# Powers as three 8-bit parts for the decay masks, and a second tile pool at the same place modulo 2048

## The chip, the core and the metric

The kernel runs on one core of a Trainium2 chip. It uses five engines: TensorE (PE, with its weight loads shown apart as PEld), VectorE (DVE), ScalarE (ACT), GpSimd (POOL) and SyncE (SP, which here only issues transfers). The metric is the device time of one execution in microseconds; a kernel's time is the median of its runs.

## What is computed

Three stages in a row: a retention attention with a decay per head, and two feed-forward blocks. Cut to what matters here:

```python
# q, k, v: 2 x 8 heads x 768 x 64; lam: one decay per head, 0.97 to 0.99
Dmask = np.where(rel >= 0, lam[:, None, None] ** rel[None, :, :], 0.0)
for b in range(nb):
    intra = np.einsum('bhij,bhjd->bhid', (qb @ kb.T) * Dmask, vb)
    inter = np.einsum('bhid,bhde->bhie', qb * lam_pow, kv_state)
    out[:, :, sl] = intra + inter
    kv_state = lam_block * kv_state + (kb * rev_pow).T @ vb
x = out                                    # 1536 tokens x 512
h = x @ w_in                               # 512 -> 2048
g = np.where(h >= 1, h, np.where(h <= -1, 0, (h + 1) ** 2 / 4))
x = g @ w_out
return ((x @ w_a) * (x @ w_b)) @ w_out2    # 512 -> 1536 -> 512
```

All of it is in 32 bits. The kernel takes attention in chunks of 128 tokens, so its masks hold powers of lam from 0 to 127.

## The kernel before

The kernel writes down every operation as a step with the engines that can do it, a cost for each, and the buffers that it reads and writes (`Plan.step`). `Plan.place` then gives each step an engine, a start and a buffer, by these costs and by a due time that follows from TensorE's steps; the program is emitted in that order, and the hardware follows it with semaphores. A change of costs or steps near the start therefore plans the whole program anew.

The buffers: 26 + 8 working tiles ("t" and "early", 128x512 32-bit words), 40 tiles for operands of products ("r"), 4 for raw weights ("raw"), three activation blocks ("block"), 7 banks of PSUM ("ps"). When attention is over, the 8 early tiles are given back, and eight more operand tiles ("late") take their place: early and late are the second pool. Between the first tiles and the second pool lie small constants, each a column of 64 bytes (`column`).

At the start the kernel makes its tables. GpSimd raises lam to exponents that lie along the partitions (`power`, L408): partitions 0 to 31 hold lam^c, 32 to 63 lam^(16c), 64 to 95 lam^(c-16) with zeros where c < 16 (L413 to L415, on VectorE). Tiles of ones and zeros (`ones_where`, `near` and `far`, L419 to L437, made by VectorE from an iota of GpSimd) pick for each key position its power: TensorE multiplies a 32x128 piece of such a tile with the 32x8 powers, 8 times into bank f1 (the far table), 16 times each into f2 and f3 (the near tables), L464 to L471. One more product spreads powers for the queries over all partitions (bank bt, L472). ScalarE copies f1 and bt out; `masks` (L483 to L493) makes from f1, f2 and f3 the two masks on VectorE and GpSimd; `query_powers` (L495) fills the query table on GpSimd.

`warm` (L510) offers 40 filler steps, each of two products of a zero tile with 512 columns; the plan puts as many where TensorE would stand idle before the first feed-forward product ends, and drops the rest. They write into a bank that they share with others. Attention then runs over twelve chunks: scores (L530), masked scores (`att_mask`), state update, output (`att_out`), and from the fifth chunk on it is interleaved with the first feed-forward products, which are "wide": 128x128 weights, 512 columns, twelve to a group. From about 99 us on only wide products are left.

Helpers record most operations, so many have one line: all products L347, two-operand instructions L328, copies and casts L332, loads L343. Operand names in a row are output<-moving operand,weights for products.

Of the kernel before, what the change touches and what calls it, by code (L numbers as in the profile page):

```python
# [9 lines left out]
F32 = mybir.dt.float32  # L10
F32R = mybir.dt.float32r
BF16 = mybir.dt.bfloat16
# [68 lines left out]
class Plan:  # L81
# [56 lines left out]
    def place(self, free, late, closes, ends, lookahead, reserve):  # L138
# [7 lines left out]
        lag, port, dma, side = 0.0, {"DVE": 0.0, "POOL": 0.0}, 0.0, 0.0  # L146
# [58 lines left out]
        while waiting:  # L205
# [24 lines left out]
            if len(way) > 3:  # L230
                if e == "SP":
                    dma = max(dma, begin + 1.4) + way[3] / 375e3
                    s.end = dma + 0.5
                else:
                    side = max(side, begin + 1.4) + way[3] / 190e3
                    dma = max(dma, begin + 1.4) + way[3] / 375e3
                    s.end = side + 0.5
            else:
                s.end = s.done + (0.2 if e == "PE" else 0.0)
# [27 lines left out]
def retention_ffn_kernel(ctx: ExitStack, tc: tile.TileContext, lam, att, w1i, w1o, w2ab, w2o, out):  # L267
# [104 lines left out]

    def column(name, dtype=F32):
        return View(fixed([128, 16], dtype, name))

    def small(e, o, ins, emit, cost=0.17, **kw):
# [3 lines left out]
    lamb, kdf, powers = column("lamb").of(lambda t: t[:, 0:H]), column("kdf").of(lambda t: t[:, 0:H]), column("powers")  # L380
    half, qi, ci, qf, cf, ef, keep, pi, dg = (
        column(n, I32 if n in ("qi", "ci", "pi") else F32)
        for n in ("half", "qi", "ci", "qf", "cf", "ef", "keep", "pi", "dg")
    )
    one = lambda v: v.of(lambda t: t[:, 0:1])
    rows32 = lambda v, i, n=1: v.of(lambda t: t[32 * i:32 * (i + n)])
    powers8 = powers.of(lambda t: t[:, 0:H])
    idle = new().of(lambda t: t.bitcast(BF16)[:, 0:512])
    load(lamb, bass.AP(tensor=lam.tensor, offset=lam.offset, ap=[[0, 128], [1, H]]), 4096, [("ACT", 2.2, False, 4096)])
    small("POOL", one(qi), [], lambda: nc.gpsimd.iota(one(qi)(), pattern=[[0, 1]], base=0, channel_multiplier=1), 0.14)  # L390
    small("DVE", idle, [], lambda: nc.vector.memset(idle(), 0.0), 0.3)
    small("DVE", one(ci), [one(qi)],
          lambda: ts_(out=one(ci)(), in0=one(qi)(), scalar1=31, scalar2=None, op0=ALU.bitwise_and))
    small("DVE", one(cf), [one(ci)], lambda: nc.vector.tensor_copy(one(cf)(), one(ci)()))
    small("DVE", one(qf), [one(qi)], lambda: nc.vector.tensor_copy(one(qf)(), one(qi)()))

    def exponents():
        nc.vector.tensor_copy(one(ef)(), one(cf)())
        x, y = (one(v)()[32:64] for v in (ef, cf))
        ts_(out=x, in0=y, scalar1=16.0, scalar2=None, op0=ALU.mult)  # L400
        x, y = (one(v)()[64:96] for v in (ef, cf))
        ts_(out=x, in0=y, scalar1=-16.0, scalar2=0.0, op0=ALU.add, op1=ALU.max)

    small("DVE", one(ef), [one(cf)], exponents, 0.51)

    def power(o, e):
# [3 lines left out]
    power(powers8, ef)  # L410
    power(kdf, qf)
    small("DVE", one(keep), [one(cf)],
          lambda: ts_(out=one(keep)(), in0=one(cf)(), scalar1=16.0, scalar2=None, op0=ALU.is_ge))  # L413
    small("DVE", powers8, [powers8, one(keep)],
          lambda: ts_(out=powers8()[64:96], in0=powers8()[64:96], scalar1=one(keep)()[64:96], scalar2=None, op0=ALU.mult))  # L415
# [3 lines left out]
    def ones_where(pattern, base, dtype=F32):  # L419
        n = new()  # L420
        whole = i_(n)
        small("POOL", whole, [], lambda: nc.gpsimd.iota(whole(), pattern=pattern, base=base, channel_multiplier=0), 0.7)

        def equal(shift):
            o, c = new(), column(f"c{base}_{shift}")
            small("DVE", one(c), [one(cf)],
                  lambda: ts_(out=one(c)(), in0=one(cf)(), scalar1=float(-shift), scalar2=None, op0=ALU.add))
            plan.step([("DVE", dve())], [o], [whole, one(c)],
                      lambda e: ts_(out=o(), in0=whole(), scalar1=one(c)(), scalar2=None, op0=ALU.is_equal))
            return o  # L430

        return equal

    equal = ones_where([[1, 4], [0, 8], [1, 16]], 1)
    near = [equal(4 * g) for g in range(4)]
    equal = ones_where([[1, 4], [1, 8], [0, 16]], -8)
    far = [equal(4 * g) for g in range(2)]  # L437
# [11 lines left out]
    def numbers():  # L449
        nc.gpsimd.iota(wi()[:, 0:8], pattern=[[1, 8]], base=32, channel_multiplier=0)  # L450
        nc.gpsimd.iota(wi()[:, 8:24], pattern=[[1, 16]], base=1, channel_multiplier=0)
# [8 lines left out]
    small("DVE", spread, [powers8, held], lambda: nc.vector.tensor_tensor(  # L460
        out=by_head(spread()[:, 0:192]), in0=powers8().rearrange("p (h o) -> p h o", o=1).to_broadcast([128, H, 24]),
# [3 lines left out]
    for o, q, sel in ((f1, 1, far), (f2, 0, near), (f3, 2, near)):  # L465
        kws = []
        for i in range(4 * len(sel)):
            kws.append(dict(out=o.of(lambda t, i=i: t[:, i * H:(i + 1) * H]),
                            lhsT=sel[i // 4].of(lambda t, i=i, q=q: t[32 * q:32 * q + 32, (i % 4) * 128:(i % 4 + 1) * 128]),
                            rhs=rows32(powers8, q), start=True, stop=True))  # L470
        mm(kws, 0.07 * len(kws), [o], [powers8, *sel])  # L471
    mm([dict(out=cols(bt, 0, 192), lhsT=full.of(lambda t: t[0:64, 0:128]), rhs=spread.of(lambda t: t[0:64, 0:192]),  # L472
             start=True, stop=True)], 0.35, [bt], [full, spread])
# [29 lines left out]

    masks(0)
# [470 lines left out]
```

## Time and profile before

| | |
|---|---|
| median of 3 runs | 614.87 us (614.62 to 616.12) |
| the profiled execution | 615.42 us |
| its span, first to last instruction | 613.6 us |
| TensorE busy | 602.4 us, 98% |
| VectorE, ScalarE, GpSimd busy | 63%, 46%, 74% |
| DMA queue of the loads | 50.86 MB, 24.1% of 16 engines' span |

TensorE is busy for nearly the whole span, and the other engines are not. Records of products overlap: a product's duration holds its way through the array, so the distance of one group's start to the next is the time that the group costs. Idle time of the other engines costs nothing unless TensorE waits for them. The "granted clock" of the views is the share of TensorE's full clock of 2.4 GHz.

### The profile page before, as it was taken

To read this page: it belongs to the slowest core of one execution; us is meant where nothing else is said; L and a number is where in the kernel's file an instruction comes from. 1 tells how busy PE (TensorE), PEld (TensorE's weight loads), DVE (VectorE), ACT (ScalarE), POOL (GpSimd) and SP (SyncE) were. 2 spreads that over 40 slices of the span, in tenths; PEclk is the share of its full clock that TensorE was granted. 3 is DMA by queue.
4 is the path that set the end of the run, shared out by engine and by line. 5 is a ranking of instruction groups with operands and counts; after the bars stand their busy time and mean duration, and the time that the engine had idled before them with its cause. 6 is when DMAs were issued, how large, how long until landed. Compare 5 with 4: busy or idle time off the path is not lost.

```text
span 613.6 us, 8555 instructions
## 1 busy us (share of the span) xinstructions
PE 602.4 (98%) x3140; PEld 494.8 (81%) x3140; DVE 389.4 (63%) x621; ACT 283.7 (46%) x498; POOL 453.2 (74%) x397
## 2 busy tenths in 40 slices
PE   6999999999999999999999999999999999999996
PEld 5887878888888888888888888888888888888885
DVE  3378884515897588677887645463873774764454
ACT  0064655644854375337766465431542542542410
POOL 4277579996979496949799999774777778768730
PEclk9999999999999999999999999999999999999999
DMA  8446530120403041304023221211121212210006
GB/s 296 182 143 240 193 136 17 69 68 2 137 19 120 1 138 34 104 0 138 0 70 109 98 68 69 69 35 34 70 73 66 69 68 69 69 70 0 1 35 204
DMA packets 19193, 51.93 MB, mean 85 GB/s; under 512 B 2256, under 2 KB 3280, under 8 KB 19152
## 3 DMA queue, kind: packets, MB, share of 16 engines
q1 hardware_dynamic: 18432, 50.86, 24.1%
q10 hardware_dynamic: 720, 0.53, 0.3%
q8 instruction: 24, 0.39, 0.3%
q14 instruction: 17, 0.14, 0.1%
HBM read 48.24 MB, written 3.15 MB: 84 GB/s over the span
## 4 chain that ended last, share of the span: by engine, by line
PE 98%; DMA 1%; DVE 0%; issue 0%; SPq 0%; DVEq 0%
PE ps L347 98%; DMA t<-in_att 1%; DVE t L328 0%; SPq L343 0%; DVEq L971 0%; DVEq L328 0%
## 5 line engine op out<-in xcount | busy, mean ns | idle before, releaser
L347 PE MATMUL ps<-r,r 128*128 128x512 f32 x984 | 270.1, 390 | 0.0
L328 POOL TENSOR_TENSOR r<-t,r 128x512 fp32r<-128x512 f32 x152 | 195.7, 1304 | 79.6 <-ACT r L332 74.6
L328 DVE TENSOR_TENSOR t<-t,ps 128x512 f32<-128x512 f32 (+1 forms) x240 | 158.5, 668 | 145.3 <-PE ps L347 126.5
L347 PEld LDWEIGHTS ps<-r,r 128*128 128x128 f32 x984 | 184.8, 188 | 40.1 <-issue 0.2
L347 PE MATMUL ps<-block,r 128*128 128x512 f32 x892 | 216.3, 391 | 0.0
L347 PEld LDWEIGHTS ps<-block,r 128*128 128x128 f32 x892 | 166.8, 188 | 36.1 <-issue 0.5
L328 POOL TENSOR_TENSOR t<-t,t 128x512 int32<-128x512 int32 (+2 forms) x140 | 152.8, 1104 | 14.6 <-DVE t L648 8.7
L332 ACT CAST r<-t 128x512 fp32r<-128x512 f32 x162 | 99.1, 619 | 137.0 <-DVE t L328 74.8
L347 PE MATMUL ps<-late,r 128*128 128x512 f32 x238 | 86.3, 394 | 0.0
L332 ACT COPY t<-ps 128x512 f32<-128x512 f32 (+3 forms) x58 | 33.0, 569 | 82.2 <-PE ps L347 81.7
L643 DVE TENSOR_SCALAR words<-words 128x512 f32<-128x512 f32 x68 | 47.2, 695 | 28.9 <-ACT words L638 28.5
L638 ACT ACTIVATE words<-raw 128x512 f32<-128x512 f32 x68 | 43.2, 636 | 36.5 <-DVE t L648 36.1
L347 PEld LDWEIGHTS ps<-late,r 128*128 128x128 f32 x238 | 44.6, 188 | 10.2
L645 DVE TENSOR_SCALAR words<-words 128x512 int32<-128x512 int32 x68 | 47.4, 697 | 1.6
L648 DVE SCALAR_TENSOR_TENSOR t<-raw,words 128x512 int32<-128x512 int32 x67 | 45.8, 684 | 2.2
L681 ACT ACTIVATE t<-t,half 128x512 f32<-128x512 f32 x45 | 32.3, 723 | 27.8 <-DVE t L679 27.7
L640 ACT ACTIVATE t<-raw 128x512 int32<-128x512 uint32 x66 | 41.8, 665 | 0.0
L347 PE MATMUL ps<-t,t 64*128 64x128 f32 (+3 forms) x504 | 33.3, 279 | 6.6 <-DMA t<-in_att 6.0
L347 PEld LDWEIGHTS ps<-t,t 128*64 128x64 f32 (+2 forms) x504 | 28.1, 159 | 11.8 <-issue 9.3
L347 PE MATMUL ps<-r,late 128*128 128x512 f32 x92 | 34.9, 397 | 0.0
L679 DVE TENSOR_SCALAR t<-ps 128x512 f32<-128x512 f32 x39 | 26.9, 689 | 12.2 <-PE ps L347 10.2
L347 PE MATMUL ps<-block,late 128*128 128x512 f32 x116 | 30.9, 395 | 0.0
(91 smaller groups left out, 358.9 us busy)
## 6 DMA issues: line engine op xcount, KB each, us to landing
raw<-in_w2ab SPq DMA_DIRECT2D x24, 512.0 KB, 3.3
t<-in_att SPq DMA_DIRECT2D x42, 256.0 KB, 4.7
raw<-in_w1i SPq DMA_DIRECT2D x16, 512.0 KB, 4.0
raw<-in_w1o SPq DMA_DIRECT2D x16, 512.0 KB, 3.4
raw<-in_w2o SPq DMA_DIRECT2D x12, 512.0 KB, 3.4
out<-t SPq DMA_DIRECT2D x8, 256.0 KB, 2.0
early<-in_att SPq DMA_DIRECT2D x6, 256.0 KB, 5.8
out<-t SPq DMA_DIRECT2D x4, 128.0 KB, 1.7
```

The source lines that it names most:

```text
L328: plan.step(ways, [o], [x, y], lambda e: engine[e].tensor_tensor(out=o(), in0=x(), in1=y(), op=op))
L332: (nc.scalar.copy if e == "ACT" else nc.vector.tensor_copy)(o(), x())
L347: return lambda e: nc.tensor.matmul(**{k: v() if isinstance(v, View) else v for k, v in kw.items()})
L638: lambda e: nc.scalar.activation(out=words(), in_=f_(high)(), func=ACTF.Abs), horizon)
L640: lambda e: nc.scalar.activation(out=c(), in_=low.of(lambda t: t.bitcast(U32))(), func=ACTF.Copy, scale=2.0**-29), horizon)
L643: lambda e: ts_(out=words(), in0=words(), scalar1=HIGH_MIN, scalar2=HIGH_MAX, op0=ALU.max, op1=ALU.min))
L645: lambda e: ts_(out=wi(), in0=wi(), scalar1=3, scalar2=0x3FFFFFFF, op0=ALU.logical_shift_left, op1=ALU.bitwise_and))
L648: lambda e: nc.vector.scalar_tensor_tensor(out=vi(), in0=high(), scalar=-0x40000000, in1=wi(), op0=ALU.bitwise_and, op1=ALU.bitwise_or))
L679: lambda e: ts_(out=r(), in0=ps(), scalar1=-1.0, scalar2=1.0, op0=ALU.max, op1=ALU.min))
L681: lambda e: nc.scalar.activation(out=r(), in_=r(), func=ACTF.Square, scale=0.5, bias=half()[:, 0:1]))
```

## The change

Every power is now written as a sum of three 16-bit numbers: the nearest one (top), the nearest to what is left (mid), and the rest. All powers for the near tables are lam^c on partitions 0 to 95, the same 32 of them three times; VectorE keeps top on partitions 0 to 31, mid on 32 to 63 and the rest on 64 to 95 (`three_parts`, seven small instructions). Partitions 96 to 127 hold lam^(16k) in the same way, eight at a time, for the far table. The products are as many as before, 8 + 16 + 16, but with 16-bit operands, and 96 or 32 partitions deep; each sums the three parts. In place of zeroed powers f3 gets four tiles of its own with other shifts, so there are ten tiles of ones and zeros instead of six; they are 16-bit. The product for the queries is 128 partitions deep instead of 64. The plan's numbers change: transfers at 400 instead of 375 KB/us and not before 4.2 us, lam's load 3.7 instead of 2.2, other costs for the new steps. At the end a tile "pad" fills the columns to a multiple of 2048 bytes.

```diff
-        lag, port, dma, side = 0.0, {"DVE": 0.0, "POOL": 0.0}, 0.0, 0.0
+        lag, port, dma, side = 0.0, {"DVE": 0.0, "POOL": 0.0}, 4.2, 4.2
...
-                    dma = max(dma, begin + 1.4) + way[3] / 375e3
+                    dma = max(dma, begin + 1.4) + way[3] / 400e3
...
     power(powers8, ef)
     power(kdf, qf)
-    small("DVE", powers8, [powers8, one(keep)],
-          lambda: ts_(out=powers8()[64:96], in0=powers8()[64:96], scalar1=one(keep)()[64:96], scalar2=None, op0=ALU.mult))
...
+            o = new().of(lambda t: t.bitcast(BF16)[:, 0:512])
+            plan.step([("DVE", 0.5)], [o], [whole, one(number)],
+                      lambda e, o=o, s=s: ts_(out=o(), in0=whole(), scalar1=float(s), scalar2=one(number)(), op0=ALU.add,
+                                              op1=ALU.is_equal))
...
-    near = [equal(4 * g) for g in range(4)]
-    far = [equal(4 * g) for g in range(2)]
+    far = ones_where([[1, 4], [1, 8], [0, 16]], -8, kf, (0, 4))
+    near = ones_where([[1, 4], [0, 8], [1, 16]], 1, cf, (0, 4, 8, 12, -16, -12, -8, -4))
...
+    def three_parts():
+        stt = nc.vector.scalar_tensor_tensor
+        nc.vector.tensor_copy(top(), powers())
+        nc.vector.tensor_tensor(out=rest(), in0=powers(), in1=top(), op=ALU.subtract)
+        nc.vector.tensor_copy(mid(), rest())
+        nc.vector.tensor_tensor(out=rest2(), in0=rest(), in1=mid(), op=ALU.subtract)
+        ts_(out=cut1(), in0=top(), scalar1=one(is_part[0])(), scalar2=None, op0=ALU.mult)
+        stt(out=cut2(), in0=mid(), scalar=one(is_part[1])(), in1=cut1(), op0=ALU.mult, op1=ALU.add)
+        stt(out=parts(), in0=rest2(), scalar=one(is_part[2])(), in1=cut2(), op0=ALU.mult, op1=ALU.add)
...
-    for o, q, sel in ((f1, 1, far), (f2, 0, near), (f3, 2, near)):
+    for o, a, b, sel in ((f1, 96, 128, [far[s] for s in (0, 4)]), (f2, 0, 96, [near[s] for s in (0, 4, 8, 12)]),
+                         (f3, 0, 96, [near[s] for s in (-16, -12, -8, -4)])):
...
-                            rhs=rows32(powers8, q), start=True, stop=True))
-        mm(kws, 0.07 * len(kws), [o], [powers8, *sel])
+                            rhs=parts.of(lambda t, a=a, b=b: t[a:b]), start=True, stop=True))
+        mm(kws, 0.08 * len(kws), [o], [parts, *sel])
...
+    const.tile([128, -len(columns) % 32 * 16], F32, name="pad")
```

TensorE's queue near its start, before (t_66 and t_68 are chunk 0, t_69 and t_71 chunk 1, ps_137 is f1):

```order
L347 MATMUL ps_136<-t_66,t_68 128x128
L347 MATMUL ps_137<-powers,t_72 128x8 x4
L347 MATMUL ps_137<-powers,t_76 128x8 x4
L347 MATMUL ps_138<-t_69,t_71 128x128
L347 MATMUL ps_139<-t_69,t_71 128x128
```

The same place after (t_70 and t_71 are chunk 1, ps_139 is f1):

```order
L347 MATMUL ps_137<-t_70,t_71 128x128
L347 MATMUL ps_138<-t_70,t_71 128x128
L347 LDWEIGHTS t_74
L347 MATMUL ps_139<-parts,t_74 128x8
L347 LDWEIGHTS t_74
```

The products for f1 stood between the scores of chunk 0 and chunk 1; now all mask products stand behind the scores of both, each with a weight load of its own.

TensorE's queue where the tables end and the fillers begin, before (ps_141 is f3, early_146 the query powers, early_147 the zero tile):

```order
L347 MATMUL ps_141<-powers,t_86 128x8 x4
L347 MATMUL ps_141<-powers,t_89 128x8 x4
L347 MATMUL ps_137<-early_146,t_65 128x192
L347 LDWEIGHTS early_147
L347 MATMUL ps_140<-early_147 128x512
```

After (early_147 is the last tile of ones and zeros, early_149 the query powers, early_151 the zero tile):

```order
L347 LDWEIGHTS early_147
L347 MATMUL ps_141<-parts,early_147 128x8
L347 MATMUL ps_139<-early_149,t_65 128x192
L347 LDWEIGHTS early_151
L347 MATMUL ps_140<-early_151 128x512
```

The order of the stages is the same; 14 fillers followed before, 10 follow now, and attention behind them in both.

VectorE's queue around the powers, before:

```order
L429 TENSOR_SCALAR t_76<-t_67,c-8_4_174 128x512
L413 TENSOR_SCALAR keep<-cf 128x1
L427 TENSOR_SCALAR c_0_169<-cf 128x1
L427 TENSOR_SCALAR c_4_170<-cf 128x1
L427 TENSOR_SCALAR c_8_171<-cf 128x1
L427 TENSOR_SCALAR c_12_172<-cf 128x1
L415 TENSOR_SCALAR powers<-powers,keep 32x8
L429 TENSOR_SCALAR t_81<-t_70,c_0_169 128x512
```

After:

```order
L428 TENSOR_SCALAR t_89<-t_69,cf 128x512
L428 TENSOR_SCALAR early_145<-t_69,cf 128x512
L447 CAST top<-powers 128x8
L448 TENSOR_TENSOR rest<-powers,top 128x8
L449 CAST mid<-rest 128x8
L450 TENSOR_TENSOR rest_161<-rest,mid 128x8
L451 TENSOR_SCALAR cut_162<-top,is_178 128x8
L452 SCALAR_TENSOR_TENSOR cut_163<-mid,is_179,cut_162 128x8
L453 SCALAR_TENSOR_TENSOR parts<-rest_161,is_180,cut_163 128x8
L428 TENSOR_SCALAR early_147<-t_69,cf 128x512
```

Two comparisons over 512 columns stood ahead of the first instruction that reads the powers, now nine do, and the powers pass seven small instructions instead of one.

## Rows read from the trace of the kernel before

**Rows 1.** The page: chain that ended last, shares of the span by engine.

```profile
PE 98%; DMA 1%; DVE 0%; issue 0%; SPq 0%; DVEq 0%
```

**Rows 2.** Waits of TensorE: who waited for whom, total us, times, longest.

```profile
PE ps L347 <- DVE t L328: 0.6, 1, 0.6
```

**Rows 3.** Timeline of TensorE: start us, us, engine, line, operation, names, shapes, count.

```profile
6.01 2.08 PE L347 MATMUL ps<-t,t 64*128 64x128 f32 x16 [6.01 <-DMA t<-in_att]
8.02 3.58 PE L347 MATMUL ps<-powers,t 32*128 32x8 f32 x16
11.53 2.08 PE L347 MATMUL ps<-t,t 64*128 64x128 f32 x16
13.53 12.99 PE L347 MATMUL ps<-powers,t 32*128 32x8 f32 x64
26.45 1.00 PE L347 MATMUL ps<-early,t 64*128 64x192 f32 x2
27.39 5.21 PE L347 MATMUL ps<-early 128*128 128x512 bf16 x14
32.52 0.69 PE L347 MATMUL ps<-t,early 128*64 128x64 f32 x16
...
41.22 1.16 PE L347 MATMUL ps<-early,early 64*128 64x128 f32 x16
...
45.45 3.03 PE L347 MATMUL ps<-block,r 128*128 128x512 f32 x12
```

**Rows 4.** Timeline of weight loads, same columns, at the first fillers.

```profile
27.39 0.10 PEld L347 LDWEIGHTS <-early 128*128 128x128 bf16 x1 [0.44 <-DVE t L490]
...
27.79 0.15 PEld L347 LDWEIGHTS <-early 128*128 128x128 bf16 x1 [0.27 <-issue]
28.22 0.15 PEld L347 LDWEIGHTS <-early 128*128 128x128 bf16 x1 [0.28 <-issue]
```

**Rows 5.** Groups by form, busy us and mean ns: 27.38 to 31.1, then 31.56 on.

```profile
L347 PE MATMUL ps<-early 128*128 128x512 bf16 x9 | 4.0, 631 | 0.0
...
L347 PE MATMUL ps<-early 128*128 128x512 bf16 x5 | 1.4, 409 | 0.0
```

**Rows 6.** Busy time in one stretch; the last column is DMA in GB/s.

```profile
12.00:20.00 8.00, 8.00 (x50) 7.78 (x48) 0.00 (x0) 0.00 (x0) 0.65 (x1) 1.00 1.04 404
```

**Rows 7.** Timeline of all engines, 0 to 10 us: VectorE and GpSimd at the tables.

```profile
5.12 1.66 POOL L408 TENSOR_TENSOR powers<-lamb,ef 128x8 f32<-128x8 f32 x1 [2.75 <-DMA lamb<-in_lam]
...
7.07 1.68 DVE L429 TENSOR_SCALAR t<-t,c 128x512 f32<-128x512 int32 x4
...
8.92 0.20 DVE L441 TENSOR_SCALAR dg<-pi 128x8 f32<-128x8 int32 x1
```

**Rows 8.** Timeline of VectorE and of GpSimd, 26 to 32 us: masks.

```profile
26.56 1.29 DVE L490 TENSOR_TENSOR t<-dg,ps 128x512 f32<-128x512 f32 x2 [4.65 <-PE ps L347]
...
29.07 2.47 DVE L328 TENSOR_TENSOR t<-ps,early 128x512 f32<-128x512 f32 x4
...
27.33 1.27 POOL L328 TENSOR_TENSOR early<-early,t 128x512 f32<-128x512 f32 x1 [14.68 <-DVE t L490]
28.55 2.63 POOL L500 TENSOR_TENSOR t<-t 64x512 f32<-64x512 f32 x2
```

**Rows 9.** TensorE: two timeline rows, then groups by form (busy us, mean ns).

```profile
142.12 4.24 PE L347 MATMUL ps<-block,r 128*128 128x512 f32 x18
...
157.20 4.34 PE L347 MATMUL ps<-block,late 128*128 128x512 f32 x18
...
L347 PE MATMUL ps<-late,r 128*128 128x512 f32 x238 | 86.3, 394 | 0.0
L347 PE MATMUL ps<-r,late 128*128 128x512 f32 x92 | 34.9, 397 | 0.0
L347 PE MATMUL ps<-block,late 128*128 128x512 f32 x116 | 30.9, 395 | 0.0
```

**Rows 10.** Timeline of SyncE: its next load after the first batch.

```profile
26.55 0.33 SPq L343 DMA_DIRECT2D t<-in_att  x1
```

More of the change, by code (lines that the diff above doesn't have):

```diff
@@ L379, in retention_ffn_kernel @@
     ts_ = nc.vector.tensor_scalar
[L380 to L383, printed above, removed]
-    )
-    one = lambda v: v.of(lambda t: t[:, 0:1])
-    rows32 = lambda v, i, n=1: v.of(lambda t: t[32 * i:32 * (i + n)])
-    powers8 = powers.of(lambda t: t[:, 0:H])
+    one = lambda v: v.of(lambda t: t[:, 0:1])
@@ new lines, in retention_ffn_kernel @@
+    eight = lambda v: v.of(lambda t: t[:, 0:H])
+    lamb, kdf, powers, rest, rest2, cut1, cut2 = (eight(column(n)) for n in ("lamb", "kdf", "powers", "rest", "rest2", "cut1", "cut2"))
+    top, mid, parts = (eight(column(n, F32).of(lambda t: t.bitcast(BF16))) for n in ("top", "mid", "parts"))
+    half, qi, ci, ki, pi, qf, cf, kf, ef, part, dg = (
+        column(n, I32 if n in ("qi", "ci", "ki", "pi", "part") else F32)
+        for n in ("half", "qi", "ci", "ki", "pi", "qf", "cf", "kf", "ef", "part", "dg")
+    )
@@ L394, in retention_ffn_kernel @@
-    small("DVE", one(cf), [one(ci)], lambda: nc.vector.tensor_copy(one(cf)(), one(ci)()))
-    small("DVE", one(qf), [one(qi)], lambda: nc.vector.tensor_copy(one(qf)(), one(qi)()))
     def exponents():
+        last = lambda v: one(v)()[96:128]
+        ts_(out=one(ci)(), in0=one(qi)(), scalar1=31, scalar2=None, op0=ALU.bitwise_and)
+        nc.vector.tensor_copy(one(cf)(), one(ci)())
         nc.vector.tensor_copy(one(ef)(), one(cf)())
[L399 to L402, printed above, removed]
@@ L404, in retention_ffn_kernel @@
-    small("DVE", one(ef), [one(cf)], exponents, 0.51)
+        ts_(out=one(ki)(), in0=one(qi)(), scalar1=7, scalar2=None, op0=ALU.bitwise_and)
+        nc.vector.tensor_copy(one(kf)(), one(ki)())
+        ts_(out=last(ef), in0=last(kf), scalar1=16.0, scalar2=None, op0=ALU.mult)
+        nc.vector.tensor_copy(one(qf)(), one(qi)())
+    small("DVE", [one(v) for v in (ci, cf, ki, kf, ef, qf)], [one(qi)], exponents, 1.0)
     def power(o, e):
@@ L419, in ones_where @@
-    def ones_where(pattern, base, dtype=F32):
+    def ones_where(pattern, base, number, shifts):
         n = new()
         whole = i_(n)
[L422 to L432, printed above, removed]
@@ new lines, in ones_where, with part_masks @@
+        return found
+    far = ones_where([[1, 4], [1, 8], [0, 16]], -8, kf, (0, 4))
+    near = ones_where([[1, 4], [0, 8], [1, 16]], 1, cf, (0, 4, 8, 12, -16, -12, -8, -4))
+    def part_masks():
+        last = lambda v: one(v)()[96:128]
+        ts_(out=one(part)(), in0=one(qi)(), scalar1=5, scalar2=None, op0=ALU.logical_shift_right)
+        ts_(out=last(part), in0=last(qi), scalar1=3, scalar2=3, op0=ALU.logical_shift_right, op1=ALU.bitwise_and)
+        for m in range(3):
+            ts_(out=one(is_part[m])(), in0=one(part)(), scalar1=m, scalar2=None, op0=ALU.is_equal)
@@ new lines, in retention_ffn_kernel @@
+    small("DVE", [one(v) for v in (part, *is_part)], [one(qi)], part_masks, 0.6)
+    def three_parts():
[7 more added lines that the diff above has]
+        stt(out=parts(), in0=rest2(), scalar=one(is_part[2])(), in1=cut2(), op0=ALU.mult, op1=ALU.add)
@@ L439, in diagonal @@
+    small("DVE", [top, mid, rest, rest2, cut1, cut2, parts], [powers, *(one(v) for v in is_part)], three_parts, 1.3)
     def diagonal():
```

31 lines of the change are left out of this document (16 added, 15 removed).

## The prediction

> **What bounds the kernel now.** I read the chain that ended last first: it is TensorE for 98% of the span [rows 1]. The waits of TensorE come next, and there are two: 6.0 us for the first attention tiles [rows 3] and 0.6 us for VectorE [rows 2]. So between 6.01 us and the end TensorE works without a break, and only what makes its own queue shorter, or slower, moves the time. The timeline of TensorE says where there is something to shorten [rows 3]. After the scores of chunk 0 it spends 8.02 to 11.53 us on the first eight mask products, 11.53 to 13.53 on the scores of chunk 1, 13.53 to 26.45 on the other 32 mask products, 26.45 to 27.39 on the product that spreads the query powers, 27.39 to 32.52 on 14 fillers, and from 32.52 on it does attention. The mask products cost 3.51 + 12.92 = 16.43 us for 40 products of eight columns, 0.41 us each.
>
> The clock belongs to this picture. The granted clock that the views print is 1.00 in all of these stretches, but the trace holds no record of it ahead of its first change, and durations say more. The fillers have 512 columns; two of their weight loads stand 0.43 us apart (27.79 and 28.22 us), which is 512 columns at 1.2 GHz [rows 4]. Up to 31.1 us a filler lasts 631 ns on the mean, after 31.56 us 409 ns [rows 5]: the clock rose to 2.4 GHz inside the fillers, after 25 us in which TensorE was busy throughout at 1.2 GHz. The scores show the same: 2.08 us for a chunk at 6.01 and 11.53, 1.16 us for the same shape at 41.22 [rows 3]. So everything ahead of 31.5 us is at the lower level, and the fillers are what lies ahead of the rise.
>
> **The change part by part.** All sums are made against the profiled execution, 615.42 us with a span of 613.60; the median of the runs shown, 614.87, lies 0.55 below it, and I subtract the same differences from the median.
>
> *Mask products.* Removed: 40 products of 32-bit powers, 16.43 us. Added: 40 pairs of a 16-bit weight load (128 columns) and a product of eight columns. The trace has no such pair. From above it is bounded by the old product's records: 16.43 us over 80 loads and products is 0.205 us, 8.2 us for 40. From below by the smallest work at the higher clock: 16 loads and products of 64 columns in 0.69 us, 0.043 us each [rows 3], 1.7 us for 40. The nearest row is the one 16-bit weight load of 128 columns that queues behind nothing, 0.10 us at the lower clock [rows 4]; I take that as the pair's pace, 40 x 0.10 = 4.0 us. Saved: 16.4 - 4.0 = 12.4 us, with ends of 8.2 and 14.7. It is all on the path, since TensorE waits for nothing there.
>
> The Trainium skill ("TensorE: Matmul & The Clock Gate", section "LDWEIGHTS (loading the stationary operand)") has a load's time go by its columns alone, 107 ns for 128 at the lower clock, and its section "Weight-path perf modes" says that loads of 128 columns that aren't 32-bit take about half. By the second, as an estimate, 40 loads are 2.1 us and the sum is 1.9 us lower; no run here shows it.
>
> *What must be ready for them.* The first eight now stand behind the scores of chunk 1, so both chunks' scores run from 6.01 to about 10.0 us. Their tiles are the third and fourth loads; 256 KB at the 404 GB/s seen from 12 to 20 us [rows 6] is 0.65 us, so they land some 1.3 us behind the first two, ahead of 8.0. The powers arrive from GpSimd at 5.12 + 1.66 = 6.78 us [rows 7]. VectorE then needs seven dependent small steps for the parts; one such step took 0.20 us (8.92 us) [rows 7], so 1.4 us, and the parts are there at 8.2 us if VectorE is free. Ahead of them in its queue now stand nine comparisons instead of two; four of them took 1.68 us [rows 7], 0.42 each, and I count 0.44. Thirteen small steps of 0.15 to 0.20 us from 1.0 us on bring it to 3.3, nine comparisons to 7.3, the parts to 8.7, still 1.3 us ahead of TensorE. If a comparison with 16-bit output cost the 0.62 us of a two-operand instruction (four in 2.47 us) [rows 8], it would be 10.3, and TensorE would wait 0.3 us; everything else of TensorE is queued behind that wait. I take nothing. The fillers write into the bank of the second mask group, which VectorE has to read first: that group ends at about 12.4, its two readers take 1.3, and the fillers start at 14.9, so this wait stays hidden.
>
> *Spreading product.* 128 rows deep now, the same 192 columns: 0.94 us stays 0.94.
>
> *Fillers.* 10 instead of 14. All ten at the lower clock are 4.27 us against 5.13 now: -0.9. If the clock rises half way they are 3.2, -1.9.
>
> So attention starts at 6.01 + 4.0 (scores) + 4.0 + 0.94 + 4.27 = 19.2 us instead of 32.52: 13.3 earlier.
>
> *Does attention keep up with it?* The chain behind the masks moves along: now the near products end at 26.45, VectorE masks them at 26.56, GpSimd adds at 27.33, and the masked scores are done at 29.07 + 2.47 = 31.5, 1.0 us ahead of 32.52; the two instructions for the query powers on GpSimd end at 31.2 [rows 8]. After, the near products end at 14.0; 1.3 us of masking and 1.3 us of adding give 16.6, two masked scores 17.9, and the query powers 16.6 + 2.6 = 19.2, while the first product that reads masked scores stands 1.2 us behind 19.2. They just make it, as now. SyncE waits for the buffers of mask tiles (ten instead of six) before it loads further chunks, but these come free with the products at 14 us, where now its next load stands at 26.55 [rows 10]. The first 17 attention tiles and four weight tiles are 6.6 MB, as now, 16 us at 404 GB/s [rows 6]. I cost all of this at nothing; if cover is gone, it shows as waits of TensorE in the first 30 us of attention, and I allow 4 us for that in the range.
>
> *Second pool.* Products that touch a tile of the second pool run slower now: 18 of one form took 4.34 us with weights from there and 4.24 us with weights from the first pool, 5.6 ns each; 238 + 116 + 92 = 446 products touch it [rows 9], 446 x 5.6 = 2.5 us, on the path. Eighteen columns of 64 bytes lie between the pools now, which puts the second 1152 bytes off the place of the first, modulo 2048; after the change it is on it. That the offset is the cause isn't shown; the ends are 2.5 and 0, and I take 2.5, because the slowing goes with the tile, whichever operand it is and whatever stands next to it.
>
> Sum: 615.42 - 12.4 - 0.9 - 2.5 = 599.6 for the profiled execution, 614.87 - 15.8 = 599.1 for the median.
>
> **The rivals.**
>
> *Fast weight loads.* The pair runs near 0.043 us even at the lower clock: another 2.3 us, 596.8. For it: the load that I took for the price is a latency, and loads may overlap products. Against: the old records don't overlap, 0.205 us each. Chance 0.17. The skill's section on weight-path modes speaks for this case.
>
> *The offset isn't the cause.* The second pool stays slow by its place or its use: 599.1 + 2.5 = 601.6. Chance 0.15. This is also the case in which that part of the change doesn't do what it says.
>
> *Attention starves.* The new order is planned afresh, the tail of the mask chain has no spare, and TensorE waits 2 to 5 us between 20 and 80 us: 601 to 604. Or the pairs cost the upper bound, 603.3. Against: one wait of 0.6 us in all of attention now. Chance 0.15 together.
>
> *The clock rises late.* Fewer fillers lie ahead of attention, and the rise may miss them. Attention up to the first wide products, 32.52 to 45.45 us now [rows 3], then takes twice its 12.93 us: 612.0. Chance 0.04. For it: 25 us of busy TensorE didn't raise the clock. Against: the rise came 4.1 us into the fillers, and ten of them with the spreading product are 5.2.
>
> *Slower.* The same, but the clock stays low even through wide products: the first group of twelve (3.03 us at 45.45 [rows 3]) gives 615.0, no change; with a second one like it, it is 618.0. That is the point: from the second group on the kernel is slower. Against: wide products keep the clock up for the rest of the run. Chance 0.03 for slower, 0.02 for the point of no change.
>
> **How the numbers follow.** My forecast, the clock up within a microsecond of the fillers' end, has 0.44: 599.1, with its own bounds of 597.5 and 600.8. The rivals have 0.17, 0.15, 0.15, 0.04 and 0.05. The range is to leave out no more than 2 in 10: 596.0, under the fast loads, to 604.0, over the starving case; the late clock and the ends of other cases are left out. A measurement of this kernel can tell about 0.3%, 1.8 us. Faster by more than that are all cases up to 612.0: 0.95; within it 0.02; slower 0.03.
>
> **What the changed profile would show.** Right: 40 pairs in some 4 us from about 10 us on, fillers from 15 us on with a mean duration that halves inside them, attention from about 19 us, no wait of TensorE over 1 us behind 20 us, and products with tiles of the second pool as far apart as others (4.24 us for 18). Wrong: a wait for VectorE in front of the pairs; scores of chunk 2 that take 2.08 us rather than 1.16 (late clock); waits for DMA, GpSimd or VectorE between 20 and 80 us; 4.34 us for 18 products with the second pool.

## The result, and the profile after

The changed kernel takes 594.89 us (median of 4 runs, 594.74 to 595.95) where the kernel before took 615.09 beside it (4 runs, 614.62 to 616.12). The ratio is 0.9673, with a 95% interval of 0.9656 to 0.969. The forecast was 599.1 with a range from 596.0: the direction was right and the two causes of the gain were the ones named, but their sizes were not, and the time came out 1.1 us below the range. The profiled execution took 594.74 us with a span of 593.0.

The timeline of TensorE in the changed kernel, with the columns of [rows 3]:

```profile
6.03 3.78 PE L347 MATMUL ps<-t,t 64*128 64x128 f32 x32 [6.03 <-DMA t<-in_att]
9.74 1.10 PE L347 MATMUL ps<-parts,t 32*128 32x8 bf16 x32
10.71 0.35 PE L347 MATMUL ps<-parts,early 96*128 96x8 bf16 x8
11.13 0.98 PE L347 MATMUL ps<-early,t 128*128 128x192 f32 x2
12.80 3.50 PE L347 MATMUL ps<-early 128*128 128x512 bf16 x10 [0.69 <-DVE t L505]
16.23 0.69 PE L347 MATMUL ps<-t,early 128*64 128x64 f32 x16
```

The mask products ran from 8.02 to 11.53 and from 13.53 to 26.45 us before [rows 3]; now all 40 stand between 9.74 and 11.13 us, 1.39 us in all. The fillers start at 12.80 behind a wait of 0.69 us for VectorE that was not there before, and attention starts at 16.23 instead of 32.52. The waits of TensorE, which answer to [rows 2], hold that new one and nothing else that is new:

```profile
PE ps L347 <- DMA t<-in_att: 6.0, 1, 6.0
PE ps L347 <- DVE t L505: 0.7, 1, 0.7
PE ps L347 <- DVE early L328: 0.6, 1, 0.6
```

What ends last there is seen in the chain of work that ended last, in order of time (start us, us, what). Its first pieces, which in the kernel before were TensorE itself from 6.01 us on:

```profile
5.21 2.58 POOL powers L413
...
9.26 0.41 DVE early L428
9.67 0.94 DVE early L474
...
12.06 0.69 DVE t L505
...
12.80 38.95 PE ps L347 x474
```

So up to the fillers the bound is no longer TensorE but the tables: the powers on GpSimd, then VectorE's queue from the parts to the readers of the second mask group. The scores hide the first part of it, and the mask products themselves lie beside it. Their pace no longer sets when the fillers start.

The fillers by form, first from 12.8 to 15.1 us, then from 15.4 to 16.3 (they answer to [rows 5]; one of the ten, in which the clock rose, stands in both):

```profile
L347 PE MATMUL ps<-early 128*128 128x512 bf16 x6 | 2.6, 610 | 0.7 <-DVE t L505 0.7
...
L347 PE MATMUL ps<-early 128*128 128x512 bf16 x5 | 1.4, 414 | 0.0
```

The clock rose some 2.4 us into them, where it took about 4 us before; the first half is at 1.2 GHz, the second at 2.4 GHz.

The wide products, grouped by form over the whole span, of the kernel before (the two groups that [rows 9] leaves out) and then of the changed one:

```profile
L347 PE MATMUL ps<-r,r 128*128 128x512 f32 x984 | 270.1, 390 | 0.0
L347 PE MATMUL ps<-block,r 128*128 128x512 f32 x892 | 216.3, 391 | 0.0
```

```profile
L347 PE MATMUL ps<-r,r 128*128 128x512 f32 x919 | 250.8, 389 | 0.0
L347 PE MATMUL ps<-block,r 128*128 128x512 f32 x836 | 206.1, 390 | 0.0
L347 PE MATMUL ps<-late,r 128*128 128x512 f32 x215 | 70.0, 389 | 0.0
L347 PE MATMUL ps<-r,late 128*128 128x512 f32 x157 | 52.8, 389 | 0.0
L347 PE MATMUL ps<-block,late 128*128 128x512 f32 x172 | 46.5, 389 | 0.0
```

Products with a tile of the second pool were 394 to 397 ns long before [rows 9] and are 389 now, like the largest group. The two groups that hold no such tile went from 390 to 389 and from 391 to 390.

So the 20.68 us between the two profiled executions (615.42 and 594.74) stand as follows; each line is a difference of starts in the two timelines, and only the last but one is what remains of the span:

| Stretch | before, us | after, us | difference |
|---|---|---|---|
| first attention tiles arrive | 6.01 | 6.03 | +0.02 |
| scores of two chunks | 4.01 | 3.71 | -0.30 |
| mask products | 16.43 | 1.39 | -15.04 |
| spreading product | 0.94 | 0.98 | +0.04 |
| wait for VectorE ahead of the fillers | 0 | 0.69 | +0.69 |
| fillers | 5.13 | 3.43 | -1.70 |
| from attention's start to the end of the span | 581.08 | 576.77 | -4.31 |
| outside the span | 1.82 | 1.74 | -0.08 |

### The profile page after: what moved, and what is told of

Its sections match the earlier page's. It is cut to its first block, busy times and chain, and to the rows that moved or that the text cites. A ratio compares the mean times of both kernels' runs of the same rounds, so it can differ in the third digit from the quotient of the medians.

```text
span 593.0 us, 8465 instructions
## 1 busy us (share of the span) xinstructions
PE 581.0 (98%) x3096; PEld 478.8 (81%) x3096; DVE 393.1 (66%) x631; ACT 282.7 (48%) x497; POOL 454.0 (77%) x397
## 4 chain that ended last, share of the span: by engine, by line
PE 97%; DVE 1%; DMA 1%; POOL 0%; issue 0%; DVEq 0%; POOLq 0%
PE ps L347 97%; DMA lamb<-in_lam 1%; POOL powers L413 0%; DVE t L328 0%; DVE early L474 0%; DVE t L505 0%; DVE early L328 0%; DVE early L428 0%; DVE early L478 0%; DVEq L991 0%; DVE cut L452 0%; DVE parts L453 0%; DVE top L447 0%; DVE mid L449 0%; DVE rest L448 0%
## 5 line engine op out<-in xcount | busy, mean ns | idle before, releaser
L347 PE MATMUL ps<-r,r 128*128 128x512 f32 x919 | 250.8, 389 | 0.0
L328 POOL TENSOR_TENSOR r<-t,r 128x512 fp32r<-128x512 f32 x127 | 163.9, 1299 | 67.7 <-ACT r L332 62.8
L347 PEld LDWEIGHTS ps<-r,r 128*128 128x128 f32 x919 | 172.5, 188 | 35.9 <-issue 0.2
L347 PE MATMUL ps<-late,r 128*128 128x512 f32 x215 | 70.0, 389 | 0.0
L332 ACT COPY t<-ps 128x512 f32<-128x512 f32 (+2 forms) x57 | 32.8, 576 | 54.0 <-PE ps L347 53.6
L347 PE MATMUL ps<-r,late 128*128 128x512 f32 x157 | 52.8, 389 | 0.0
L328 POOL TENSOR_TENSOR late<-t,r 128x512 fp32r<-128x512 f32 x26 | 33.7, 1296 | 19.5 <-ACT r L332 19.5
L347 PE MATMUL ps<-block,late 128*128 128x512 f32 x172 | 46.5, 389 | 0.0
L328 POOL TENSOR_TENSOR r<-t,late 128x512 fp32r<-128x512 f32 x27 | 35.5, 1324 | 4.0 <-ACT late L332 2.6
L347 PEld LDWEIGHTS ps<-block,late 128*128 128x128 f32 x172 | 32.3, 188 | 6.7
```

Of the source, the lines that this page charges most:

```text
L328: plan.step(ways, [o], [x, y], lambda e: engine[e].tensor_tensor(out=o(), in0=x(), in1=y(), op=op))
L332: (nc.scalar.copy if e == "ACT" else nc.vector.tensor_copy)(o(), x())
L347: return lambda e: nc.tensor.matmul(**{k: v() if isinstance(v, View) else v for k, v in kw.items()})
```

## The experiments

Four questions: is the slow second pool a matter of its place, and of which distance; what the mask products' gain rests on; what the fillers are worth; and why VectorE was late.

**The pad alone, in the kernel before.** Fourteen columns of 64 bytes more put the second pool on the place of the first, modulo 2048, and nothing else changes.

```diff
-    masks(0)
+    const.tile([128, 14 * 16], F32, name="pad"); masks(0)
```

> The kernel before with a pad of 896 bytes behind its columns, so that the second pool lies at the first's place modulo 2048; nothing else is changed. Theory (offset): every wide product stands 226 to 227 ns from the next, and the time falls from 615.1 by 4.2 us (the 4.3 us by which the stretch from the first state product to the end got shorter with the whole change) to 610.9. My own sum had 2.5 us: 612.6. Rival (the offset is not the cause): 615.1.

Measured: 611.03 us (610.77 to 611.43) against 615.45, ratio 0.9928 (0.9913 to 0.9943). Its products by form:

```profile
L347 PE MATMUL ps<-r,r 128*128 128x512 f32 x984 | 269.1, 389 | 0.0
L347 PE MATMUL ps<-block,r 128*128 128x512 f32 x892 | 215.9, 390 | 0.0
L347 PE MATMUL ps<-late,r 128*128 128x512 f32 x238 | 85.1, 389 | 0.0
```

The counts are those of the kernel before, the durations those of the changed one. The place is the cause, and it is worth 4.4 us. By the means, 5 ns on 238 products, 8 on 92 and 6 on 116 are 2.6 us. The two groups that hold no tile of the second pool were busy 1.0 and 0.4 us less (270.1 to 269.1 and 216.3 to 215.9), so 1.4 us of the gain lies in products that only stand near the others. Taken from each product's start to the next, all wide products of this trace together lost 4.36 us, about 3.0 of it where a tile of the second pool is used.

**The change without its pad.** The second pool then lies 24 columns of 64 bytes, 1536 bytes, off the first.

```diff
-    const.tile([128, -len(columns) % 32 * 16], F32, name="pad")
```

> The changed kernel without the pad tile alone, so the second pool lies 1536 bytes past the first modulo 2048 and nothing else moves. Theory (the offset slows products with a tile of the second pool, and their neighbours too): such products stand 232 to 234 ns apart instead of 227, and the time is some 4 us longer than the changed kernel's 594.9, about 599. Rival (the second pool was slow by its use, and the new plan uses it otherwise): 227 ns everywhere and 594.9.

Measured: 595.12 us (594.98 to 595.99), the same as with the pad. The products by form, one group:

```profile
L347 PE MATMUL ps<-late,r 128*128 128x512 f32 x215 | 70.0, 389 | 0.0
```

So not every offset slows them, 1152 bytes does and 1536 doesn't; the theory that any does fell. The line that the change adds for this is not what brings the gain here: the new number of columns would have done.

**Three more distances.** The pad is made larger, so that the offset becomes 128, 256 or 64 bytes.

```diff
-    const.tile([128, -len(columns) % 32 * 16], F32, name="pad")
+    const.tile([128, 8 * 16 + 32], F32, name="pad")
```

(64 in place of 32 for 256 bytes, 16 for 64 bytes.)

> The changed kernel with 128 bytes more of pad: the second pool lies 128 bytes past the first modulo 2048. The run with 1536 bytes was not slowed, the kernel before with 1152 was; 1536 is a multiple of 512, and 1152 is 128 past one. Theory (the place modulo 512 decides): products with a tile of the second pool stand 232 to 234 ns apart, 599. Rival (modulo 2048 only some places hurt, 1152 among them, small ones not): 227 ns and 595.

> The same with 256 bytes instead of 128. Theory (modulo 512): slowed, 599. Rival (modulo 256): 227 ns and 595.

> The changed kernel with 64 bytes more of pad. Offsets of 0, 256 and 1536 bytes were not slowed, 128 and 1152 were: the place modulo 256 counts. Theory (only that, and 64 is off it too): products with a tile of the second pool stand over 230 ns apart, 598 to 602. Rival (only the far half of a 256-byte place hurts, or 64-byte steps are free): 227 ns and 595.

Measured: 602.47, 595.89 and 603.28 us, one run each, on chips where the kernel before took 615.34, 615.34 and 615.75. The products by form, of the offset of 128 bytes, then of 256, then of 64:

```profile
L347 PE MATMUL ps<-r,r 128*128 128x512 f32 x919 | 252.7, 391 | 0.0
...
L347 PE MATMUL ps<-late,r 128*128 128x512 f32 x215 | 70.9, 393 | 0.0
...
L347 PE MATMUL ps<-block,late 128*128 128x512 f32 x172 | 47.7, 397 | 0.0
L347 PE MATMUL ps<-late,late 128*128 128x512 f32 x41 | 14.9, 395 | 0.0
```

```profile
L347 PE MATMUL ps<-late,r 128*128 128x512 f32 x215 | 70.0, 389 | 0.0
```

```profile
L347 PE MATMUL ps<-r,r 128*128 128x512 f32 x919 | 253.1, 392 | 0.0
...
L347 PE MATMUL ps<-late,r 128*128 128x512 f32 x215 | 71.2, 395 | 0.0
```

Not slowed at 0, 256 and 1536 bytes; slowed at 64, 128 and 1152. All six fit "the same place modulo 256", and modulo 512 fell at 256 bytes. The times are 7.6 and 8.4 us above the changed kernel's, but 1 us of that is the clock: in all three of these executions it rose later (17.6 to 18.2 us instead of 15.2) and attention started at 17.1 instead of 16.2. Beside the run with 256 bytes, which has this too and took 595.89, the wrong place costs 6.6 and 7.4 us. Products without a tile of the second pool are 2 to 3 ns longer too. The runs moved only the second pool, so they don't separate "the same place as the first pool" from "a multiple of 256 bytes" by itself; that products with both operands in the second pool are slowed as well (395 ns, the last line at 128 bytes) speaks for the latter. Why, no run shows.

**32-bit masks in the new order.** Everything of the change but the 16-bit operands: the tiles of ones and the last sum of the three parts are kept in 32 bits.

```diff
-    top, mid, parts = (eight(column(n, F32).of(lambda t: t.bitcast(BF16))) for n in ("top", "mid", "parts"))
+    top, mid = (eight(column(n, F32).of(lambda t: t.bitcast(BF16))) for n in ("top", "mid")); parts = eight(column("parts"))
...
-            o = new().of(lambda t: t.bitcast(BF16)[:, 0:512])
+            o = new()
```

> The changed kernel with its parts and its tiles of ones and zeros in 32 bits; same plan, same order, pad kept. Theory (the width of the operands makes the mask products dear): a product takes 0.4 us at the lower clock again instead of 0.027, 40 x 0.38 = 15 us, of which 0.7 is covered by the wait for VectorE in front of the fillers: 609. Rival (the new order and plan made the gain, not the width): under 598.

Measured: 609.29 us (607.87 to 610.73) against 615.45, ratio 0.9899 (0.9876 to 0.9923). TensorE's timeline:

```profile
9.59 11.16 PE L347 MATMUL ps<-parts,t 32*128 32x8 f32 x64
20.61 3.56 PE L347 MATMUL ps<-parts,early 96*128 96x8 f32 x16
24.02 0.99 PE L347 MATMUL ps<-early,t 128*128 128x192 f32 x2
```

Here the 40 products take 14.43 us, 0.36 each, against 0.41 before [rows 3] and 0.035 with 16-bit operands. The type of the operands is the larger part of the whole change: 14.4 of the 20.2 us go with this one edit. Of the 6.2 us by which this run still beats the kernel before, 4.4 are the pool's, so the new order, the deeper products and the four fillers less leave under 2 us. With this run's median the share is blurred by the clock. In the profiled execution, which took 608.01 us, it rose at 9.32 us and fell at 12.73 while TensorE was busy throughout, so the first 14 of the 40 ran at 2.4 GHz: the records of these products, two for each, start 0.112 us apart there and 0.213 behind it, and 0.213 in the kernel before. At the same clock a product cost what it did before. The four runs are two pairs, 607.87 and 608.01 with a mean granted clock of 0.986, and 610.57 and 610.73 with 1.000. If the second pair had the low clock throughout the mask products, as these figures suggest but no trace of it shows, the type is worth 15.8 us, and the new order, the deeper products and the fewer fillers together 0.4.

**Weights in two halves.** Each mask product is split into two with 64 columns of weights each.

```diff
+            for c in (0, 64):
+                kws.append(dict(out=o.of(lambda t, i=i, c=c: t[c:c + 64, i * H:(i + 1) * H]),
+                                lhsT=sel[i // 4].of(lambda t, i=i, a=a, b=b, c=c: t[a:b, (i % 4) * 128 + c:(i % 4) * 128 + c + 64]),
```

> The changed kernel with each of the 40 mask products split into two with 64 columns of weights, so 80 pairs of a load and a product. Theory (the 27 ns per pair come from a load mode for 128 columns of 16 bits, as the Trainium skill's page 'TensorE: Matmul & The Clock Gate', section 'Weight-path perf modes', has it): without that mode 64 columns take 53 ns at 1.2 GHz, 80 pairs 4.3 us instead of 1.1, and the masks end 3 us later, of which 0.7 is covered. Rival (a pair's price goes with its columns, or is a fixed 27 ns): 1.1 to 2.2 us for the 80.

Measured: 595.16 us, one run. TensorE's timeline:

```profile
9.71 1.44 PE L347 MATMUL ps<-parts,t 32*64 32x8 bf16 x64
11.00 0.40 PE L347 MATMUL ps<-parts,early 96*64 96x8 bf16 x16
11.33 0.59 PE L347 MATMUL ps<-early,t 128*128 128x192 f32 x2
```

80 pairs take 1.62 us where 40 took 1.39, and that moved nothing, as it must where the tables are the bound. But the clock rose at 10.23 us in this execution, inside them. The first sixteen, still at 1.2 GHz, lie 0.40 us from the first start to the last, where the eight whole ones of the changed kernel lie within 0.21. So a split pair costs about twice a whole one at the same clock, and a price that goes with the columns falls. The halves of a pair write different columns and rows of the output, so they may have run side by side, and the run doesn't tell whether the two halves cost a fixed price each or run side by side without the mode of the theory. That stays open.

**Without fillers.**

```diff
-    warm(40)
+    warm(0)
```

> The changed kernel without any filler (they compute nothing that is used), planned again. Theory (the fillers raise the clock, and attention's own products don't, as the 25 us of busy TensorE at 1.2 GHz before them showed): attention up to the first wide products runs at 1.2 GHz, 13 us of it take 26, and 3.4 us of fillers fall away: 601 to 606. Rival (attention's products raise the clock soon): the first masked scores still end at 16.4 us, so attention can't start its outputs earlier, and the time is 594 to 596.

> The changed kernel without any filler once more, beside the run above. Theory (attention's own products raise the clock, and the mask chain on VectorE, not TensorE, is late at the start, so low clock there costs little): 592.8 within 0.5, wherever the clock rises. Rival (the first time was lucky in where the clock rose): 594 and more, or runs that differ by several us.

Measured: 592.83 us (592.73 to 593.56), ratio 0.9636 (0.962 to 0.9652), 2.06 below the change; run again beside other variants, 592.98 (592.78 to 593.96), ratio 0.9632 (0.9618 to 0.9645). Both theories of the first run missed: the theory by 8 us, its rival by 1.2. TensorE's timeline in the first:

```profile
12.57 0.69 PE L347 MATMUL ps<-t,early 128*64 128x64 f32 x16 [0.88 <-POOL t L565]
13.06 1.82 PE L347 MATMUL ps<-t,t 128*64 128x64 f32 x32
15.62 0.43 PE L347 MATMUL ps<-t,t 128*64 128x128 f32 x2 [0.74 <-DVE t L328]
```

and in the second, the same program:

```profile
12.57 1.12 PE L347 MATMUL ps<-t,early 128*64 128x64 f32 x16 [0.46 <-POOL t L565]
13.45 6.26 PE L347 MATMUL ps<-t,t 128*64 128x64 f32 x64
```

Attention starts 3.66 us earlier, behind GpSimd's scaling of a chunk, and gives some of that back. In the first execution the clock rose at 10.32 us, in the mask products, and attention is at the high clock at once (0.49 us for sixteen products of 64 columns, as after the fillers), and the 0.9 us more that TensorE then waits for VectorE are part of the price. In the second it runs at the low clock: 0.88 us for the same sixteen, 6.19 us until the next group for 64 that take 3.4 at the pace of the changed kernel. The clock rises in attention by itself, at 18.75 us. The chain that ended last leads through the tables in the first execution, and in the second through a load of attention tiles and GpSimd's scaling behind it (5.94 to 12.53 us). The late rise didn't cost the 12.9 us of my rival: the second execution took 593.95 us, the three shortest of this program 592.78 to 592.98, so about 1.1 us.

**VectorE's late instruction.** The wait ahead of the fillers is for VectorE's first reader of the second mask group. VectorE's timeline in the changed kernel:

```profile
9.03 0.23 DVE L453 SCALAR_TENSOR_TENSOR parts<-rest,is,cut 128x8 bf16<-128x8 f32 x1
...
9.59 1.00 DVE L474 TENSOR_SCALAR early<-t,qf 128x24 f32<-128x24 int32 x1
...
11.46 0.68 DVE L505 TENSOR_TENSOR t<-early,ps 128x512 f32<-128x512 f32 x1
```

and GpSimd's:

```profile
5.21 2.57 POOL L413 TENSOR_TENSOR powers<-lamb,ef 128x8 f32<-128x8 f32 x1 [2.73 <-DMA lamb<-in_lam]
...
9.47 1.09 POOL L565 TENSOR_TENSOR early<-t,kdf 128x512 f32<-128x512 f32 x1
```

The small comparison at L474 took 1.00 us and ends at 10.59; GpSimd's scaling, which began just before it, ends at 10.56. The powers took GpSimd 2.57 us instead of 1.66 [rows 7]; the last of VectorE's nine comparisons over 512 columns ran beside them until 6.27 us. To test whether the first costs time, the comparison is moved ahead of all this, without fillers:

```diff
+    def part_masks_and_held():
+        part_masks()
+        ts_(out=held()[:, 0:24], in0=wi()[:, 0:24], scalar1=one(qf)(), scalar2=None, op0=ALU.is_equal)
...
+    small("DVE", [*(one(v) for v in (part, *is_part)), held], [one(qi), which, one(qf)], part_masks_and_held, 0.8)
```

> No fillers, and VectorE's comparison over 24 columns (which lasted 1.00 us at 9.6 us, while GpSimd ran its scaling of keys from 9.46 to 10.55) moved ahead of the 512-column comparisons, where GpSimd only runs iotas. Theory (VectorE waited there for a port that GpSimd held): 0.2 us instead of 1.0, the masks and attention 0.7 us earlier, 592.1. Rival (the instruction is slow of itself, or something else is late by as much): 592.8, as without fillers alone.

Measured: 593.11 us (592.65 to 593.94), as without the move. VectorE, then GpSimd:

```profile
2.62 0.23 DVE L454 TENSOR_SCALAR t<-t,qf 128x24 f32<-128x24 int32 x1
...
9.73 1.18 DVE L481 TENSOR_TENSOR early<-powers,t 128x192 f32<-128x192 f32 x1
```

```profile
9.61 1.09 POOL L568 TENSOR_TENSOR early<-t,kdf 128x512 f32<-128x512 f32 x1
```

The comparison takes 0.23 us where nothing of GpSimd runs. The next instruction of VectorE stalls in its place, 1.18 us instead of 0.36, and again ends just behind GpSimd's. So it isn't this instruction; both lost their time beside the scaling. In this execution the chain ahead of attention led through a load and GpSimd's scaling (5.89 to 12.42 us), not through VectorE, so the run can't price the stall. The Trainium skill ("SBUF — State Buffer", section "SBUF: two separate sides") has some instructions of VectorE and those of GpSimd take one pair of ports in turn, each for its whole length; the two pairs of ends, 10.59 by 10.56 and 10.91 by 10.70, agree with it. Another row doesn't: in the kernel before the same two instructions took 0.23 and 0.36 us at 9.03 and 9.29, inside GpSimd's power for the keys (8.89 to 10.53 us). So it depends on what GpSimd runs, and the measurement decides. Nor does every instruction of VectorE lose: the two mask readers at 11.46 and 12.06 us, with one operand in PSUM, took their usual 0.68 us beside the next scaling (11.47 to 12.51).

The other way round: three of the comparisons wait for the powers, so that fewer run beside GpSimd while it computes them (again without fillers).

```diff
-            plan.step([("DVE", 0.5)], [o], [whole, one(number)],
+            plan.step([("DVE", 0.5)], [o], [whole, one(number), *([powers] if s in (-12, -8, -4) and base == 1 else [])],
```

> No fillers, and three of VectorE's ten 512-column comparisons made to wait for the powers, so that fewer of them run while GpSimd raises the powers. Theory (the 512-column comparisons hold a port that GpSimd needs, which is why the powers took 2.57 us instead of the 1.66 of the kernel before): the powers take 1.7 to 2.0 us, the parts are there 0.8 us earlier, VectorE has its small steps behind it when the near products end, and the masked scores and attention come some 0.7 us earlier than without fillers alone: 592.1. Rival (the powers take long because of their new exponents, or GpSimd's next scaling stalls VectorE again): 2.6 us for the powers or a stall as long elsewhere, and 592.8.

Measured: 592.47 us (592.40 to 592.68; ratio 0.9622, 0.9608 to 0.9635), 0.51 below the median of the same kernel without the edit run beside it, and 0.3 to 0.5 below that kernel's three shorter runs; the ranges don't meet (592.78 is the other's lowest), but the margin is small. GpSimd and VectorE:

```profile
5.15 1.86 POOL L413 TENSOR_TENSOR powers<-lamb,ef 128x8 f32<-128x8 f32 x1 [2.67 <-DMA lamb<-in_lam]
```

```profile
8.27 0.23 DVE L453 SCALAR_TENSOR_TENSOR parts<-rest,is,cut 128x8 bf16<-128x8 f32 x1
...
10.68 0.67 DVE L505 TENSOR_TENSOR early<-early,ps 128x512 f32<-128x512 f32 x1
```

The powers take 1.86 us, the parts end 0.76 us earlier, and the first mask reader starts at 10.68 where it started at 11.18 without the edit. What TensorE makes of it:

```profile
12.05 0.69 PE L347 MATMUL ps<-t,early 128*64 128x64 f32 x16 [0.59 <-issue]
...
22.89 1.16 PE L347 MATMUL ps<-t,t 64*128 64x128 f32 x16 [0.30 <-DMA t<-in_att]
```

Attention starts 0.52 us earlier, and at 22.89 TensorE waits for a load instead; the chain that ended last now leads through the loads of attention's tiles, not through the tables. The edit also made the plan place other steps anew, so how much of the 0.5 us is the powers' and how much the new order's can't be said; and the clock fell in this execution at 12.67 us, in attention, and rose again at 16.08. That GpSimd's instruction is shorter with less of the comparisons beside it is plain: they end 0.32, 1.06 and 1.24 us after the powers have begun (this run, the changed kernel, the run before this one), and the powers take 0.20, 0.91 and 1.09 us more than 1.66. The second half of the rival came true as well: three comparisons took 2.07 us from 8.41 on, beside GpSimd's scaling (8.77 to 9.81), where three took 1.27 in the first run without fillers. This version, without fillers, is the shortest of all that ran.

## Why the prediction was right and wrong

*What bounds the kernel* held for the kernel before, and from the fillers on for the changed one (TensorE has 97% of its chain). Ahead of the fillers the bound passed to the tables, which the prediction had looked at and costed at nothing.

*Mask products* (forecast 4.0 us, ends 1.7 and 8.2; measured 1.39). This is the step that failed. The forecast was 4.2 us off where its range allowed 3.1 downward, and 2.6 of them are this term, the next largest part the second pool. That the products become cheap was right, but the price of a pair was taken from one load that queued behind nothing, 0.10 us [rows 4]. That is the latency of a load, not the distance at which loads follow each other: in the changed kernel each load's record is still 0.10 us long, and eight of them lie within 0.29 us (the row of weight loads below). The first 32 of the 40 take 0.97 us (9.74 to 10.71), 0.030 us each, at the low clock: the spreading product behind them takes 0.98 us, as before, and 0.56 in executions where the clock had risen by then. The row that I chose as the nearest was the wrong kind of number, and the lower end, 0.043 us from 16 products at the higher clock, was of 32-bit products and so no lower bound. The rival of fast weight loads described this case and had 0.17; its 596.8 still stopped at 0.043. The argument against it, that the old records don't overlap, was a misreading: the 80 records in [rows 3], two for each 32-bit product, are 357 ns long on the mean and start 0.21 us apart. The Trainium skill ("TensorE: Matmul & The Clock Gate", section "Weight-path perf modes") has such loads about twice as fast; the measured pace of a whole pair, 30 ns, is shorter than even half of the 107 ns that the prediction cites for a load. Off by 2.6 us.

*Scores* (4.0; measured 3.71). Off by 0.3: two chunks in one row take less than two rows of one chunk.

*What must be ready.* The attention tiles arrived in time. The row of weight loads in the changed kernel shows a small wait ahead of the masks, of the size that I priced at 0.3 us and took as nothing; it is put down to the comparison that follows the parts in VectorE's queue (9.18 to 9.67 us):

```profile
9.74 0.29 PEld L347 LDWEIGHTS <-t 32*128 32x128 bf16 x8 [0.22 <-DVE early L428]
```

It is part of the 3.71 us above. The parts were done at 9.26 us, not 8.7, because the powers took 2.57 us instead of the 1.66 that I carried over from [rows 7]: I moved seven more comparisons beside that instruction and gave it the old duration. So the 1.3 us that I gave this step as cover were used up.

*The fillers' bank wait* ("stays hidden"; measured 0.69 us). This follows from the first miss and from VectorE: the second group, products 9 to 24, ended at about 10.5 instead of 12.4, which takes cover away, and its readers began at 11.46, behind an instruction that stalled 0.8 us beside GpSimd. I had checked the wait against the forecast's own pace and not against the lower end of its range.

*Spreading product* held, 0.98 us.

*Fillers* (forecast -0.9, with -1.9 if the clock rose half way; measured -1.70). The clock rose inside them. The case was named and priced, and I took the other.

*Does attention keep up?* It did. The chain behind the masks moved with it, and no new wait stands behind 13 us in the changed kernel. The 4 us that the range allowed for it weren't needed, and they pulled the range to the wrong side.

*Second pool* (2.5; measured 4.31 in the changed kernel from attention's start on, 4.4 by the pad alone). The cause was right, and now it is shown rather than argued. The size was off by 1.8. I counted only the 446 products that name a tile of the second pool; the 1876 others of the two largest groups hold 1.4 us, which no row that I read beside each other could show without the kernel after. The rest is the price: 5.6 ns from one pair of rows, where the means of those groups fell by 5 to 8.

*The rivals.* The late clock, put at 612.0, doesn't cost that: when it came, without fillers, it was about 1.1 us: the clock rose some 6 us into attention, in the middle of its small products, and not at the first wide ones. The offset was the cause, and attention didn't starve.

In sum, of the 4.9 us between the forecast of the difference (15.8) and the measured one (20.68): mask products 2.6, pool 1.8, fillers 0.8, scores 0.3, against 0.7 for VectorE; the rest is the tiles, the spreading product and what lies outside the span.

## What to carry to other kernels

The time of a lone instruction says little on the pace of a row of them; where a trace has no row of that kind, the lower end must be far below every row of another type. Where TensorE is the bound, a table that is made with many small 32-bit products is worth rewriting as sums of 16-bit parts, and tiles that serve the same products are best kept at the same place modulo 256 bytes (where the first pool starts was never varied). Fillers should be tried again after a change, and taken out if the real work raises the clock by itself. An execution's clock is worth reading before two executions are compared.

## What the runs showed of the hardware

- Pairs of a 16-bit weight load of 128 columns and a product of eight columns follow each other after 0.030 us at 1.2 GHz (32 in 0.97 us); 32-bit ones after 0.41 us [rows 3]. At 2.4 GHz (the run without the pad, where the clock had risen at 8.84 us) the same 32 took 0.89 us, hardly less, while the records of the 32-bit products in the new order stood 0.112 instead of 0.213 us apart.
- Wide 32-bit products are 389 ns long with both pools at the same place modulo 256 bytes (offsets 0, 256, 1536) and 393 to 397 with offsets of 64, 128 and 1152; neighbours that use the first pool alone are up to 3 ns longer.
- TensorE's clock isn't set by how long TensorE has been busy: before, 25 us of it without a break were at 1.2 GHz; with 32-bit masks in the new order it rose 3.2 us into the scores (9.32 us) and fell at 12.73 us, in the midst of unbroken mask products. One program without fillers started its attention at 2.4 GHz in one execution and at 1.2 in another.
- VectorE and GpSimd slow each other: powers on GpSimd took 1.66, 1.86, 2.57 or 2.75 us by how long VectorE's comparisons ran on beside them, and an instruction of VectorE of 0.23 or 0.36 us took 1.00 or 1.18 beside GpSimd's scaling of 512 columns, but no longer than usual beside its power of eight.
